# Attention output transposed through DRAM and VectorE in 32x32 blocks, in place of TensorE

## The chip, the cores and the metric

The kernel runs on one core of one Trainium2 chip. The metric is the device time of one execution in microseconds (us), median of several. A core has TensorE (PE in the profile, with its weight loads as PEld), VectorE (DVE), ScalarE (ACT), GpSimd (POOL) and SyncE (SP). Each works through its own instructions in order. In this kernel SP computes nothing: it issues every data transfer, and the transfers are carried out by 16 DMA engines.

## The reference, cut to what matters

An mLSTM cell over 4 batches, 8 heads, 768 steps and head size 40 is followed by a feed-forward layer with a quick-GELU.

```
for t in range(768):                      # per batch and head
    m_new = max(f[t] + m, i[t])
    C = exp(f[t] + m - m_new) * C + exp(i[t] - m_new) * outer(v[t], k[t])
    n = exp(f[t] + m - m_new) * n + exp(i[t] - m_new) * k[t]
    y[t] = sigmoid(o[t]) * (C @ q[t]) / max(abs(n . q[t]), 1)
x = y as (batch*time, head*dim)           # 3072 x 320
h = x @ w_in                              # 320 x 2048
out = (h * sigmoid(1.702 * h)) @ w_out    # 2048 x 320
```

The inputs w_in and w_out are 64-bit floats that the kernel converts to 32 bits by itself.

## The kernel before, in words

Time is cut into six windows (`w`) of 128 steps (`L`), and a window holds four batches (`b`) of 128 tokens. The recurrence is worked out in chunked form, as a masked attention inside a window plus a state that is carried from window to window. For one window and batch the attention has four stages:

- `weights(w, b)`: exponentials on ACT over a tile `wt`, and a causal mask on POOL. For windows after the first, `wt` is loaded by `spread` from a DRAM copy (`m_row`) of a row of maxima.
- `scores(w, b)`: key-query products on TensorE (L329), which VectorE multiplies into `wt` (L331).
- `values(w, b)`: products of `wt` with v (L340) and of q with the state (L346) on TensorE. VectorE then takes seven operations (L350 to L360), the last of which writes `y`, 128 tokens by 320 channels.
- `seam(w, b)`: puts `y` with channels on partitions into `xT[w]`, a tile of 128 partitions by 3 channel groups by 4 batches by 128 tokens. Three TensorE transposes (L369) go into one PSUM tile, and ACT copies it out (L370). Group 2 holds channels 256 to 319 twice, because POOL has appended a second copy of the last 64 channels to `y` (L362).

Feed-forward has two phases per window. In the up phase `up(w, j)` multiplies the converted w_in (`w_in_sb` for channels 0 to 255, `w_in_x` for the others, which are held on both halves of the partitions) with all 512 tokens of `xT[w]` (L405, L411), and ACT applies the GELU. In the down phase window 0 uses plain products (`down`, 16 blocks, L432). Windows 1 to 5 use a two-level fast scheme (`down_fast`, 14 blocks of 8 products, L486) whose results VectorE adds into `o_sb` (L489, L491), and SP stores them (L495).

The order of work is written by hand, and each engine follows program order. While the down phase of window `w` runs, the attention of window `w+1` is interleaved: `attention(w+1)` is a list of eight steps. The first is `columns`. Each later step holds, in this order, `seam` of the batch three behind, `values` of the batch two behind, `scores` of the batch one behind and `weights` of the newest batch, where these exist. `stops` lists after which blocks a step is run. At block 0 of the down phase the gates (`load_gates`, 2 transfers) and the blocked keys and queries (`load_blocks`, 32 transfers) of window `w+2` are issued on SP. The VectorE transposes of these blocks (`transposes`, L288) run in the next up phase. PSUM has two pools of four tiles: `ps_m` for feed-forward, `ps_a` for attention.

Of the kernel before, what the change touches and what calls it, by code (L numbers as in the profile page):

```python
# [8 lines left out]
FP = mybir.dt.float32  # L9
# [13 lines left out]
L = 128  # L23
# [11 lines left out]
def kernel(  # L35
# [12 lines left out]
    nc = tc.nc  # L48
    B, H, S, D = q.shape
    BH = B * H  # L50
    DM = H * D
    DFF = moe_w_in.shape[1]
    NW = S // L
# [12 lines left out]
    work = ctx.enter_context(tc.tile_pool(name="work", bufs=2))  # L66
# [3 lines left out]
    rows = ctx.enter_context(tc.tile_pool(name="rows", bufs=2, space=bass.MemoryType.DRAM))  # L70
# [4 lines left out]
    V, A, G, T = nc.vector, nc.scalar, nc.gpsimd, nc.tensor  # L75
# [11 lines left out]
    w_in_sb = const.tile([128, 2, DFF], FP, name="w_in_sb")  # L87
# [8 lines left out]
    def load(w, what, bs=slice(0, B)):  # L96
        hs = slice(bs.start * H, bs.stop * H)
        for c in what:
            if c == "o" and w not in eo:
                eo[w] = ld.tile([L, BH, D], FP, tag="eo", bufs=1, name="eo")  # L100
            dst, src = {"k": (k_st, k), "q": (q_st, q), "v": (v_st, v), "o": (eo.get(w), o_gate)}[c]
            nc.sync.dma_start(out=dst[:, hs, 0:D],  # L102
                              in_=src[bs, :, w * L:(w + 1) * L, :].rearrange("b h s d -> s (b h) d"))
# [12 lines left out]


    w_in_bits, w_out_bits = moe_w_in.bitcast(U32), moe_w_out.bitcast(U32)
    rest_bits = w_in_bits[256:DM, :].rearrange("k (j two m) -> two k j m", two=2, m=256)
    out_bits = w_out_bits.rearrange("(f p) m -> p f m", p=128)  # L120

# [1 line left out]


    def piece_in(c, n):
        return (w_in_sb[:, c, n * 512:(n + 1) * 512],
                [(slice(0, 128), slice(0, 512), w_in_bits[c * 128:(c + 1) * 128, n * 1024:(n + 1) * 1024])])

    def piece_rest(n):
        return (w_in_x[:, n * 4:n * 4 + 4, :].rearrange("p j m -> p (j m)"),  # L130
# [46 lines left out]
    ident = const.tile([128, 128], FP, name="ident")  # L177
# [26 lines left out]

    m_at = {0: m0}
    cols, stacked, m_row, dec = {}, {}, {}, {}
    kT, qT, wt, ys, xT, gs, o_ps, sums = {}, {}, {}, {}, {}, {}, {}, {}


    def convert(n):  # L210
# [122 lines left out]
    def values(w, b):  # L333
        hs = slice(b * H, (b + 1) * H)
        po = ps_a.tile([L, H, D1], FP, tag="a", name="p_o")
        for p in range(NP):
            for i in range(2):
                h = 2 * p + i
                for t in HALVES:
                    T.matmul(po[t, h, :], wt[w, b][:, p, i, t], v_st[:, b * H + h, :], start=True, stop=True)  # L340
        u = po
        if w:
            pi = ps_a.tile([L, H, D1], FP, tag="a", name="p_i")
            for p in range(NP):
                for t in HALVES:
                    T.matmul(pi[t, 2 * p:2 * p + 2, :].rearrange("p a b -> p (a b)"), qT[w, b][:, p, t],  # L346
                             state[:, b * NP + p].rearrange("p a b -> p (a b)"), start=True, stop=True)
            u = work.tile([L, H, D1], FP, tag="u", name="u")
            g = cols[w][:, BH + b * H:BH + (b + 1) * H].unsqueeze(2).to_broadcast([L, H, D1])
            V.tensor_tensor(out=u, in0=pi, in1=g, op=OP.mult)  # L350
            V.tensor_tensor(out=u, in0=po, in1=u, op=OP.add)

        den = work.tile([L, H, 1], FP, tag="den", name="den")
        V.tensor_scalar(out=den, in0=u[:, :, D:D1], scalar1=-1.0, scalar2=1.0, op0=OP.mult, op1=OP.max)
        V.tensor_tensor(out=den, in0=u[:, :, D:D1], in1=den, op=OP.max)
        V.reciprocal(out=den, in_=den)
        z = eo[w][:, hs, :]
        V.scalar_tensor_tensor(out=z, in0=z, scalar=1.0, in1=u[:, :, 0:D], op0=OP.add, op1=OP.mult)
        y = ys[w, b] = work.tile([L, DM + 64], FP, tag="y", name="y")
        V.scalar_tensor_tensor(out=y[:, 0:DM].rearrange("p (h d) -> p h d", d=D), in0=z, scalar=0.5,  # L360
                               in1=den.to_broadcast([L, H, D]), op0=OP.mult, op1=OP.mult)
        G.tensor_copy(out=y[:, DM:DM + 64], in_=y[:, DM - 64:DM])  # L362

    def seam(w, b):
        if b == 0:
            xT[w] = work.tile([128, 3, B, L], FP, tag="xT", bufs=1, name="xT")
        px = ps_a.tile([128, 3, L], FP, tag="a", name="p_x")
        for c in range(3):
            T.transpose(px[:, c, :], ys[w, b][:, c * 128:(c + 1) * 128], ident)  # L369
        A.copy(out=xT[w][:, :, b, :], in_=px)  # L370

    def carry(w, b):
# [22 lines left out]
    def up(w, j):  # L395


        x = xT[w].rearrange("p c b t -> p c (b t)")
        ph = {}

        def full(j, first):
            for c in range(2):
                for i in range(2):
                    f = 2 * j + i
                    T.matmul(ph[j][i], w_in_sb[:, c, f * 128:(f + 1) * 128], x[:, c, :], start=(first and c == 0),  # L405
                             stop=(not first and c == 1))

        def rest(j, first):
            for i in range(2):
                r = slice(i * 64, i * 64 + 64)  # L410
                T.matmul(ph[j][i], w_in_x[r, j, :], x[r, 2, :], start=first, stop=not first)  # L411

        def gelu(j):
            g = gs[w, j] = gp.tile([128, 2, W], FP, tag="g", name="g")
            for i in range(2):
                A.activation(out=g[:, i, :], in_=ph[j][i], func=AF.Gelu_apprx_sigmoid)  # L416

        for j, first in ((j, True), (j + 1, False)):
            ph[j] = [ps_m.tile([128, W], FP, tag="m", name="p_h") for _ in range(2)]
            if first:  # L420
                full(j, True)
            rest(j, not first)
            if not first:
                full(j, False)
            gelu(j)
# [23 lines left out]
    def weight_sums():  # L449
        V.tensor_tensor(out=t1, in0=w01, in1=w00, op=OP.subtract)  # L450
        V.tensor_tensor(out=t2, in0=w11, in1=t1, op=OP.subtract)
        V.tensor_tensor(out=w01, in0=w11, in1=w01, op=OP.subtract)
        V.tensor_tensor(out=t4, in0=w10, in1=t2, op=OP.subtract)
# [64 lines left out]
    def run(calls):  # L518
        for f, *args in calls:
            f(*args)  # L520
# [37 lines left out]
    def weights_in(n):  # L558
        done, ahead = beside.get(n, ((), ()))
        for p in done:  # L560
            convert(p)
        for p in ahead:
            fetch(p)

    for w in range(NW):
        more = w + 1 < NW
        for j in range(NF // 2):
            if j % 2 == 0:
                if w == 0:
                    weights_in(j // 2)  # L570
                up(w, j)
            if j == 0 and more:
                load(w + 1, "o")
            if w == 0 and j == 0:
                load_blocks(1)
            if w == 1 and j == 1:
                weight_sums()
            if more:
                if j == (3 if w == 0 else 0):
                    gates(w + 1)  # L580
                if j == 4:
                    load(w + 1, "v")
                if j == (7 if w == 0 else 4):
                    spread(w + 1)
                    load(w + 1, "k")
                if j < B:
                    carry(w, j)
                if 4 <= j < 6 if w else j == 7:
                    first = 2 * j - 8 if w else 0
                    transposes(w + 1, first)  # L590
                    transposes(w + 1, first + 1)
            if w and j >= 4:
                hidden_sums(w, (j - 4,), False)
                if j % 2:
                    hidden_sums(w, (j - 5, j - 4), True)
        side = attention(w + 1) if more else []
        if w == 0:

            blocks = [(lambda b=b, n=n: down(w, b, n)) for n0 in (0, 2) for b in range(B) for n in (n0, n0 + 1)]
            stops = range(0, 16, 2)  # L600
        else:
            blocks = down_fast(w, 0) + down_fast(w, 1)
            stops = (0, 1, 2, 4, 6, 8, 10, 12)
        for i, block in enumerate(blocks):
            if w == 0:
                weights_in(4 + i)
                if i == 0:
                    transposes(1, 2)
                    transposes(1, 3)
            if w + 2 < NW and i == 0:  # L610
                load_gates(w + 2)
                load_blocks(w + 2)
            block()
            if i in stops and side:
                run(side.pop(0))
# [30 lines left out]
```

## Time and profile before

The median of three runs is 532.8 us (532.19 to 535.05); the profiled execution spans 532.6 us.

| engine | busy us | share of the span |
|---|---|---|
| PE | 513.5 | 96% |
| PEld | 352.1 | 66% |
| DVE | 266.0 | 50% |
| ACT | 168.3 | 32% |
| POOL | 70.1 | 13% |

| stretch, us from the start | what runs | PE busy us |
|---|---|---|
| 0 to 33 | attention of window 0 | 28.1 |
| 33 to 70.7 | up phase of window 0 | 37.7 |
| 70.7 to 134.6 | down phase of window 0, attention of window 1 | 53.0 |
| 134.6 to 172.4 | up phase of window 1 | 37.8 |
| 172.4 to 216.7 | down phase of window 1, attention of window 2 | 44.3 |

The later windows repeat the last two rows, and the final down phase has no attention beside it. A row of the profile's groups gives the line, the engine, the operation, the tiles it writes and reads, the shapes, the count, the busy time and the mean time of one. The timeline lists the same work in order of time: start, duration, engine, line, operation, tiles, count, and in square brackets the idle time before it and what ended that. "SPq" is SP issuing transfers; a transfer lands later than its issue ends.

### The profile page before, as it was taken

How to read it: one execution, taken by the hardware profiler on the slowest of the kernel's cores; microseconds unless marked ns; L12 is line 12 of the kernel's file. 1: busy time of each engine (PE TensorE's matmuls, PEld its weight loads, DVE VectorE, ACT ScalarE, POOL GpSimd, SP SyncE). 2: the span in 40 equal slices, each digit the busy share in tenths (PEclk: the TensorE clock that was granted, in tenths of full speed). 3: DMA queues.
4: the chain of work that ended last, by engine and by line, in shares of the span. 5: the costliest groups of instructions: out<-in, count | busy, mean ns of one | idle time of the engine just before them, and what ended most of it. 6: DMA issues, size and time to landing. Idle time of an engine off the chain costs nothing.

```text
span 532.6 us, 9546 instructions
## 1 busy us (share of the span) xinstructions
PE 513.5 (96%) x3828; PEld 352.1 (66%) x3828; DVE 266.0 (50%) x603; ACT 168.3 (32%) x367; POOL 70.1 (13%) x104
## 2 busy tenths in 40 slices
PE   8899995599999999999999999999999999999997
PEld 5654463477434999544899643899744799844797
DVE  6868962845376555237365317455307545202511
ACT  4475643520222620212540222451032352032100
POOL 5511000102130110120010220021220021000000
PEclk9999999599999999999999999999999999999999
DMA  9979689740379400387500368610357000000000
GB/s 168 138 248 326 78 153 273 78 55 26 63 210 100 52 27 1 75 220 81 59 27 1 75 171 113 76 28 2 70 102 162 0 14 15 26 0 1 1 25 26
DMA packets 175884, 44.81 MB, mean 84 GB/s; under 512 B 164544, under 2 KB 170720, under 8 KB 175840
## 3 DMA queue, kind: packets, MB, share of 16 engines
q1 hardware_dynamic: 175840, 44.21, 43.4%
q8 instruction: 30, 0.49, 0.4%
q14 instruction: 14, 0.11, 0.1%
HBM read 40.17 MB, written 4.01 MB: 83 GB/s over the span
## 4 chain that ended last, share of the span: by engine, by line
PE 78%; SPq 10%; DMA 5%; ACT 2%; DVE 2%; issue 2%; ACTq 0%
PE p_out L486 27%; PE p_h L405 27%; PE p_h L411 7%; PE p_out L432 4%; PE p_o L340 4%; SPq L113 4%; PE p_s L329 4%; SPq L154 3%; SPq L102 3%; DMA bits<-in_moe_w_in_dram 2%; PE p_i L346 2%; ACT wt L318 2%; DMA wt<-m_row 1%; PE p_x L369 1%; PE p_c L381 1%
## 5 line engine op out<-in xcount | busy, mean ns | idle before, releaser
L405 PE MATMUL p_h<-xT,w_in_sb 128*128 128x512 f32 x384 | 175.0, 602 | 0.0
L405 PEld LDWEIGHTS p_h<-xT,w_in_sb 128*128 128x128 f32 x384 | 69.8, 190 | 92.0 <-issue 89.7
L416 ACT ACTIVATE g<-p_h 128x512 f32<-128x512 f32 x96 | 54.6, 596 | 135.4 <-PE p_h L411 74.9
L486 PE MATMUL p_out<-w_out_sb,g 128*128 128x160 f32 x480 | 71.3, 302 | 0.0
L486 PEld LDWEIGHTS p_out<-w_out_sb,g 128*128 128x128 f32 x480 | 66.8, 190 | 3.7 <-issue 2.4
L321 POOL TENSOR_SCALAR_AFFINE_SELECT wt<-wt 128x1024 f32<-128x1024 f32 x24 | 26.4, 1100 | 203.7 <-ACT wt L318 194.2
L370 ACT COPY xT<-p_x 128x384 f32<-128x384 f32 x24 | 11.5, 478 | 128.7 <-PE p_x L369 128.7
L491 DVE TENSOR_TENSOR o_sb<-o_sb,p_out 128x160 f32<-128x160 f32 x70 | 21.1, 318 | 62.0 <-PE p_out L486 61.7
L318 ACT ACTIVATE wt<-wt,cols 128x128 f32<-128x128 f32 x160 | 48.0, 390 | 8.8 <-DMA wt<-m_row 8.8
L411 PE MATMUL p_h<-xT,w_in_x 64*128 64x512 f32 x192 | 47.7, 615 | 0.0
L486 PE MATMUL p_out<-t,s 128*128 128x160 f32 x320 | 47.5, 301 | 0.0
L486 PEld LDWEIGHTS p_out<-t,s 128*128 128x128 f32 x320 | 44.3, 190 | 0.6
L470 DVE TENSOR_TENSOR s<-g 128x512 f32<-128x512 f32 x20 | 13.8, 692 | 54.0 <-ACT g L416 53.6
L331 DVE TENSOR_TENSOR wt<-p_s,wt 128x512 f32<-128x512 f32 x48 | 30.8, 683 | 19.4 <-POOL wt L321 16.6
L340 PE MATMUL p_o<-v_st,wt 128*64 128x41 f32 x768 | 28.4, 235 | 11.0 <-DVE wt L331 10.9
L432 PE MATMUL p_out<-w_out_sb,g 128*128 128x320 f32 x128 | 38.4, 455 | 0.0
L390 DVE TENSOR_TENSOR state<-p_c,state 40x164 f32<-40x164 f32 x32 | 10.4, 326 | 55.1 <-PE p_c L381 54.7
L411 PEld LDWEIGHTS p_h<-xT,w_in_x 64*128 64x128 f32 x192 | 16.5, 186 | 29.5 <-issue 28.0
L340 PEld LDWEIGHTS p_o<-v_st,wt 128*64 128x64 f32 x768 | 25.3, 141 | 15.9 <-DVE wt L331 11.9
L432 PEld LDWEIGHTS p_out<-w_out_sb,g 128*128 128x128 f32 x128 | 24.9, 199 | 10.9 <-issue 2.1
L329 PE MATMUL p_s<-qT,kT 40*128 40x128 f32 x384 | 28.8, 291 | 0.0
L350 DVE TENSOR_TENSOR u<-p_i,cols 128x328 f32<-128x328 f32 x20 | 10.0, 500 | 35.6 <-PE p_i L346 35.6
(114 smaller groups left out, 524.0 us busy)
## 6 DMA issues: line engine op xcount, KB each, us to landing
wt<-m_row SPq DMA_DIRECT2D x20, 512.0 KB, 6.8
bits<-in_moe_w_in_dram SPq DMA_DIRECT2D x8, 512.0 KB, 5.1
out_dram<-o_sb SPq DMA_DIRECT2D x24, 160.0 KB, 1.8
eo<-in_o_gate_dram SPq DMA_DIRECT2D x5, 640.0 KB, 5.4
v_st<-in_v_dram SPq DMA_DIRECT2D x5, 640.0 KB, 5.8
k_st<-in_k_dram SPq DMA_DIRECT2D x5, 640.0 KB, 8.0
bits<-in_moe_w_out_dram SPq DMA_DIRECT2D x8, 320.0 KB, 4.8
k_bl<-in_k_dram SPq DMA_DIRECT2D x40, 64.0 KB, 2.6
```

The source lines that it names most:

```text
L113: nc.sync.dma_start(out=dst[r:r + 32, :, g, 0:n], in_=src[:, two:H:2, t:t + 32, d:d + n].rearrange("b j s d -> s (b j) d"))
L318: A.activation(out=x[:, h, :], in_=x[:, h, :], func=AF.Exp, scale=-1.0, bias=cols[w][:, b * H + h:b * H + h + 1])
L321: G.affine_select(out=x, in_=x, compare_op=OP.is_ge, fill=0.0, base=0, pattern=[[0, H], [1, L]], channel_multiplier=-1)
L329: T.matmul(pw[i][:, p, :], kT[w, b][r, p, :], qT[w, b][r, p, :], start=True, stop=True)
L331: V.tensor_tensor(out=wt[w, b][:, :, i, :], in0=pw[i], in1=wt[w, b][:, :, i, :], op=OP.mult)
L340: T.matmul(po[t, h, :], wt[w, b][:, p, i, t], v_st[:, b * H + h, :], start=True, stop=True)
L405: T.matmul(ph[j][i], w_in_sb[:, c, f * 128:(f + 1) * 128], x[:, c, :], start=(first and c == 0), stop=(not first and c == 1))
L411: T.matmul(ph[j][i], w_in_x[r, j, :], x[r, 2, :], start=first, stop=not first)
L416: A.activation(out=g[:, i, :], in_=ph[j][i], func=AF.Gelu_apprx_sigmoid)
L432: T.matmul(po, gs[w, f // 2][:, f % 2, b * L:(b + 1) * L], w_out_sb[:, f, :], start=(f == 0), stop=(f == NF - 1))
L486: T.matmul(po, a(f), b[:, f, :], start=(f == 0), stop=(f == NH - 1))
L491: V.tensor_tensor(out=dst, in0=x, in1=po, op=OP.add)
```

## The change

For windows 1 to 5 the transposes leave TensorE and ACT. `values` now writes `y` to a DRAM tile (`y_row`) with three transfers. It reads it back with four more into an SBUF tile `yb`, of which there is one buffer, so that four groups of 64 channels lie on four groups of 32 partitions. `seam` then makes two VectorE transposes in blocks of 32x32 from `yb` into `xT`. In this layout group 0 of `xT` holds the even and group 1 the odd channels of the first 256. The rows of w_in are therefore loaded in the same order (`full_bits`), and window 0, which keeps TensorE, transposes every second channel. POOL's copy of the last 64 channels is kept for window 0 alone. In the fast down phase the steps of the attention run after blocks 0, 1, 2, 4, 5, 7, 8 and 12 (before: 0, 1, 2, 4, 6, 8, 10 and 12), so that more blocks lie between the last `values` and the last `seam`. The loads for window `w+2` are issued at block 9 in place of block 0, in window 0 as well. The purpose is to take the transposes off TensorE.

```diff
+    full_bits = w_in_bits[0:256, :].rearrange("(p c) (n m) -> c n p m", c=2, m=1024)
...
     def piece_in(c, n):
-        return (w_in_sb[:, c, n * 512:(n + 1) * 512],
-                [(slice(0, 128), slice(0, 512), w_in_bits[c * 128:(c + 1) * 128, n * 1024:(n + 1) * 1024])])
+        return w_in_sb[:, c, n * 512:(n + 1) * 512], [(slice(0, 128), slice(0, 512), full_bits[c, n])]
...
-        G.tensor_copy(out=y[:, DM:DM + 64], in_=y[:, DM - 64:DM])
+        if w == 0:
+            G.tensor_copy(out=y[:, DM:DM + 64], in_=y[:, DM - 64:DM])
+            return
+
+        row = rows.tile([L, 4, 96], FP, tag="y_row", name="y_row")
+        nc.sync.dma_start(out=row[:, :, 0:64], in_=y[:, 0:256].rearrange("t (q m) -> t q m", q=4))
+        for i in range(2):
+            nc.sync.dma_start(out=row[:, 2 * i:2 * i + 2, 64:96],
+                              in_=y[:, 256:DM].rearrange("t (q m) -> t q m", q=2))
+        yb[w, b] = work.tile([128, 4, 96], FP, tag="yb", bufs=1, name="yb")
+        for g in range(4):
+            nc.sync.dma_start(out=yb[w, b][:, g, :], in_=row[g * 32:(g + 1) * 32].rearrange("t q m -> q t m"))
 
     def seam(w, b):
         if b == 0:
             xT[w] = work.tile([128, 3, B, L], FP, tag="xT", bufs=1, name="xT")
+        y = ys[w, b]
+        if w:
+            V.transpose(out=xT[w][:, 0:2, b, :], in_=yb[w, b][:, :, 0:64].rearrange("p g (f c) -> p c g f", c=2))
+            V.transpose(out=xT[w][:, 2, b, :], in_=yb[w, b][:, :, 64:96])
+            return
         px = ps_a.tile([128, 3, L], FP, tag="a", name="p_x")
-        for c in range(3):
-            T.transpose(px[:, c, :], ys[w, b][:, c * 128:(c + 1) * 128], ident)
+        for c in range(2):
+            T.transpose(px[:, c, :], y[:, 0:256].rearrange("p (f c) -> p c f", c=2)[:, c], ident)
+        T.transpose(px[:, 2, :], y[:, 256:384], ident)
         A.copy(out=xT[w][:, :, b, :], in_=px)
...
-            stops = (0, 1, 2, 4, 6, 8, 10, 12)
+            stops = (0, 1, 2, 4, 5, 7, 8, 12)
...
-            if w + 2 < NW and i == 0:
+            if w + 2 < NW and i == 9:
                 load_gates(w + 2)
                 load_blocks(w + 2)
```

More of the change, by code (lines that the diff above doesn't have):

```diff
@@ L206 @@
     cols, stacked, m_row, dec = {}, {}, {}, {}
-    kT, qT, wt, ys, xT, gs, o_ps, sums = {}, {}, {}, {}, {}, {}, {}, {}
+    kT, qT, wt, ys, yb, xT, gs, o_ps, sums = {}, {}, {}, {}, {}, {}, {}, {}, {}
     def convert(n):
```

## The prediction

> **What bounds the kernel now.** I read the busy times first, then a table of stretches of the span, one per phase.
>
> ```profile
> PE 513.5 (96%) x3828; PEld 352.1 (66%) x3828; DVE 266.0 (50%) x603; ACT 168.3 (32%) x367; POOL 70.1 (13%) x104
> ```
>
> ```profile
> 70.70:134.60 63.90, 52.97 (x401) 39.24 (x400) 32.55 (x68) 21.59 (x52) 8.19 (x12) 0.87 0.61 117
> 134.60:172.40 37.80, 37.80 (x162) 15.80 (x161) 23.97 (x39) 8.52 (x15) 6.62 (x4) 1.00 0.72 131
> 172.40:216.70 44.30, 44.30 (x497) 42.39 (x496) 22.43 (x58) 14.58 (x41) 7.98 (x12) 1.00 0.19 28
> ```
>
> Columns: stretch, length, busy time of PE, PEld, DVE, ACT, POOL, PE clock, DMA share, GB/s. From 134.6 us on, PE is busy in every microsecond of both phases, so each microsecond of PE work removed there is gained, and each wait that reaches PE is lost. Only the down phase of window 0 has a hole: PE works 53.0 of 63.9 us, because `wt` for window 1 comes late.
>
> Next the timeline of one step, in the down phase of window 1:
>
> ```profile
> 185.23 1.13 PE L340 MATMUL p_o<-v_st,wt 128*64 128x41 f32 x32
> 186.18 0.77 PE L346 MATMUL p_i<-state,qT 128*64 128x82 f32 x16
> 186.88 1.16 PE L329 MATMUL p_s<-qT,kT 40*128 40x128 f32 x16
> 187.00 0.50 DVE L350 TENSOR_TENSOR u<-p_i,cols 128x328 f32<-128x328 f32 x1 [1.19 <-PE p_i L346]
> ...
> 189.07 0.49 DVE L360 SCALAR_TENSOR_TENSOR y<-eo,den 128x320 f32<-128x320 f32 x1
> 189.48 1.28 DVE L331 TENSOR_TENSOR wt<-p_s,wt 128x512 f32<-128x512 f32 x2
> ...
> 192.42 0.49 PE L369 MATMUL p_x<-ident,y 128*128 128x128 f32 x3
> 192.84 1.13 PE L340 MATMUL p_o<-v_st,wt 128*64 128x41 f32 x32
> ...
> 214.51 2.34 PE L486 MATMUL p_out<-w_out_sb,s 128*128 128x160 f32 x16
> 216.69 3.60 PE L405 MATMUL p_h<-xT,w_in_sb 128*128 128x512 f32 x8
> ```
>
> `y` is ready 2.65 us after the end of the step's PE products (186.9 to 189.56), and the masked scores of the next batch, which the next `values` needs on PE, come behind it on VectorE 1.2 us later. The three transposes hold PE for 0.42 us (192.42 to 192.84). From 186.9 to the up phase at 216.69 PE takes 29.8 us.
>
> Last SP's own timeline and the issues:
>
> ```profile
> 163.53 8.33 SPq L113 DMA_DIRECT2D k_bl<-in_k_dram  x16
> 171.97 9.90 SPq L113 DMA_DIRECT2D q_bl<-in_q_dram  x16
> ```
>
> ```profile
> out_dram<-o_sb SPq DMA_DIRECT2D x24, 160.0 KB, 1.8
> k_bl<-in_k_dram SPq DMA_DIRECT2D x40, 64.0 KB, 2.6
> ```
>
> SP takes 0.52 us for one small load (8.33 over 16), and a transfer lands 1.8 us (stores) or 2.6 us (loads) after its issue. These are now hidden by early issue. The change puts two such landings in series between `values` and `seam`.
>
> **What the Trainium skill says.** "DMA: Bandwidth & Descriptors", section "Two DMAs through the same engine are not ordered": a transfer that reads what another wrote must be held back on the issuing engine until the first one's semaphore is complete. So SP stands still while `y_row` lands, and all that is behind it on SP waits. The trace of before has the same pattern once per window (`m_row`, then `wt`) but with up to 10 us between the two, so it doesn't price it. The same page, section "Why a DMA increments its semaphore by 16 and not by 1": a transfer is spread over the largest number of engines up to 16 that divides the slowest dimension of both sides. The reads of `yb` have a slowest dimension of 4 on the DRAM side, so perhaps 4 engines; no row here shows it. "VectorE: DVE Perf Modes", section "The three transpose paths": VectorE transposes 32x32 blocks only, hence the detour. "TensorE: Matmul & The Clock Gate", Part 1: an idle window of about 3.4 us halves PE's clock. The trace agrees: after the hole before 98.5 us the clock is 0.50 until about 107 us.
>
> **The change, part by part.** Removed: 20 times three transposes on PE, 0.42 us where another step follows and 0.33 us for the last of a window, so 1.6 us a window and 8 us in all. The ACT copies (0.48 us) and POOL copies (0.24 us) were hidden behind PE and count nothing. The other order of w_in rows reads the same rows in the same sizes: nothing. Window 0's strided transposes have the same count and shape: nothing.
>
> Added on VectorE: two transposes per batch, 256 and 128 columns. L288 takes 0.67 to 0.71 us for 512 columns, so about 0.5 us. VectorE is half idle, so by itself this costs nothing.
>
> Added on SP and DMA: a round trip C from `y` to a landed `yb`. Three issues of about 0.4 us (a store's issue takes 0.33 us, a load's 0.38 to 0.5 us); the third starts 0.9 us after `y` and lands 1.9 us later: 2.8 us. Then four issues 0.5 us apart, the last landing 2.5 us after its start: 4.1 us with the wake-up. C = 6.9 us; I take 7.0 for a little of the four-engine effect. Lower end: issues of 0.33 and 0.35 us, landings of 1.8 and 1.6 us (the quickest of any load): 5.1 us. Upper end: the DMA engines spent 43.4% of 16 x 532.6 us on 44.2 MB, 12 bytes per ns, so a row of 384 bytes costs 32 ns and 128 of them on each of four engines 4.1 us; with issue overlapping C is about 9 us.
>
> The wait this adds is VectorE's. `seam(b)` stands ahead of `values(b+1)` in a step, and VectorE is in order. So while `yb` of batch b is in flight, the seven operations of batch b+1, the masked scores after them and the evictions all queue up. The four batches become a chain: `y` of one batch, C, 0.5 us of transposes, 2.55 us to the next `y`. From 186.9 as zero: first `y` at 2.65, then 4 round trips, 3 times 3.05 us, the last transposes 0.5 and a wake-up 0.1: 12.4 + 4C = 40.4 us before the up phase can begin. PE alone would need 28.2 us (29.8 less 1.6). PE meets the chain where `values(2)` and `values(3)` wait for their masked scores (about 2.8 and 5 us) and before the up phase (about 4 us). The four blocks between the last `values` and the last `seam` (9 us) hide the last round trip nearly, not the three before, which fall between steps 5.0, 7.1 and 5.0 us apart. So plus 10.6 us a window, for the attention of windows 2 to 5: **+42 us**.
>
> The down phase of window 0 is worse, since its steps stand two blocks apart to the end (`stops` there is unchanged) and the 34 loads at block 9 come on SP between the row transfers of batch 1 and of batch 2. The first `y` is at 104.6 us (just ahead of VectorE's masking at 104.59). Then 104.6 + 7.0 + 3.05 = 114.7 for the second; its reads are issued by 119.7; the loads take SP 0.9 + 32 x 0.52 = 17.6 us, to 137.3, a store 0.35; third round trip lands 144.7; fourth `y` 147.8; landed 154.8; up phase at 155.4 in place of 134.6: **+21 us**. In windows 1 to 3 the loads come behind the last batch's reads and end about 15 us into the up phase. The transposes that use them start 21 us into it and `spread`'s landing is wanted after its end, so moving them costs nothing there.
>
> Clock: the hole of some 20 us before the up phase of window 1 should halve the clock as the one at 98 us did, where PE took 11.9 us (98.53 to 110.44) for about 8 us of work: **+4 us**. The holes of 3 to 5 us in the other windows may or may not, and inside the chain a slow PE is hidden: **+2 us** in all. Sum: 42 + 21 + 4 + 2 = 69, so 532.8 + 69 = **602 us**.
>
> **Rivals.** (1) The round trip is hidden and only the PE work counts: 532.8 - 8 = 525 us. For it speaks that DMA is 81% idle in the down phases; against it that 12.4 + 4C must be under 28.2, so C under 4.0 us, when two landings alone take 3.4 us at their quickest and seven issues 2.3 us. (2) C is near 4.0 and only the loads in window 0 hurt: windows 1 to 4 gain 6 us, window 0 ends 9 us later (111.7, 114.7, 132.3, 136.3, 139.4, 144): 536 us. (3) Every hole halves the clock: some 4 us more in each of four windows, 618 us. It is backed by the 0.50 after 98 us; against it the holes are half as long. (4) Four engines and C = 9: 18.6 us in each of four windows, 27 in window 0, 640 us.
>
> **How the numbers follow.** Forecast, with C between 5.1 (562 us: 3 us a window, 13 in window 0, clock 4) and 8: 0.62. Rivals (1) 0.08, (2) 0.06, (3) 0.15, (4) 0.09. The range 560 to 632 leaves out (1), (2) and about half of (4). Faster 0.08, same 0.02, slower 0.90.
>
> **What would show it.** PE idle in the down phases ended by VectorE's `wt` (L331) and, before the up phase, by VectorE's `xT`; VectorE idle ahead of its `xT` transposes ended by a DMA into `yb`, some 4 us or more each; about 10 us more in each down phase from window 1 on and 20 in that of window 0; up phases as long as before. Wrong would be a round trip under 4 us, VectorE working ahead of a waiting `seam`, or transfers of batch 2 in window 0 that don't wait for the loads.

## The result, and the profile after

The changed kernel takes 645.6 us (median of four, 642.9 to 647.8) against 532.5 us: 1.211 times as long, with an interval of 1.205 to 1.217. The profiled execution spans 641.2 us, 108.6 us more than before.

First the busy times, then the stretches from the start of window 0's down phase to the start of window 2's up phase. The columns are those of the same table of before.

```profile
PE 550.3 (86%) x3768; PEld 379.8 (59%) x3768; DVE 280.2 (44%) x643; ACT 159.2 (25%) x347; POOL 66.9 (10%) x84
```

```profile
74.00:164.70 90.70, 52.45 (x388) 38.40 (x386) 37.18 (x76) 19.69 (x48) 8.27 (x8) 0.82 0.50 99
164.70:205.50 40.80, 40.78 (x161) 17.07 (x162) 24.01 (x40) 8.52 (x15) 6.62 (x4) 0.93 0.56 105
205.50:267.80 62.30, 50.70 (x485) 47.66 (x483) 24.65 (x66) 12.67 (x37) 7.14 (x8) 0.86 0.15 34
```

PE has fewer instructions (60 transposes gone) and a larger busy time, because its clock is lower: 0.86 in the down phase of window 1, where it was 1.00. In that phase PE is now idle for 11.6 of 62.3 us. The DMA engines taken together are no busier than before, 15% of their time in this phase against 19%, so it is not the bandwidth of the 16 that is short.

The table of waits says for what the engines stood still, in us, with the number of waits and the longest:

```profile
DVE xT L380 <- DMA yb<-y_row: 148.4, 20, 20.1
PEld p_o L340 <- DVE wt L331: 55.9, 33, 8.2
PEld p_h L422 <- DVE xT L380: 36.8, 5, 22.9
```

The first line is the new wait, all 20 of it: VectorE in front of the transposes. The other two are where it reaches PE, in `values` by way of the masked scores and before the up phases. Before, the wait in `values` was

```profile
PEld p_o L340 <- DVE wt L331: 11.9, 5, 11.2
```

The chain of work that ended last shows what one batch consists of. These are batch 1 of window 2 and the start of batch 2 (start, duration, what):

```profile
235.99 0.50 DVE y L360
236.50 0.55 SPq L367
237.10 0.62 SPq L369
237.77 1.68 DMA y_row<-y
239.46 0.53 SPq L373
240.04 0.52 SPq L373
240.61 0.51 SPq L373
241.16 3.75 DMA yb<-y_row
245.04 0.45 DVE xT L380
245.49 0.19 DVE xT L381
245.68 0.40 DVE u L350
...
247.63 0.50 DVE y L360
248.15 0.55 SPq L367
```

From one `y` to the next, 236.5 to 248.1 us, there is not one entry of PE: two issues, a landing, three issues, a landing, then VectorE. In the down phase of window 1 of before the same chain was PE throughout. One step of it (the dots stand for the three transposes, 0.33 us):

```profile
188.04 4.54 PE p_out L486 x32
...
192.91 1.06 PE p_o L340 x32
193.98 0.59 PE p_i L346 x16
194.57 1.09 PE p_s L329 x16
195.66 4.54 PE p_out L486 x32
```

The round trip C, from the end of `y` to the first transpose, is 8.6 us here; the four of window 2 take 10.5, 8.6, 7.9 and 8.2 us, 8.8 in the mean.

The length of each phase, from the starts of the first products in the timeline:

| phase | before, us | changed, us | more, us | predicted, us |
|---|---|---|---|---|
| start, to the up phase of window 0 | 32.8 | 36.1 | 3.3 | 0 |
| down phase of window 0 | 63.8 | 90.7 | 26.9 | 21 |
| down phases of windows 1 to 4 | 44.3, 44.3, 44.3, 44.1 | 62.3, 61.7, 62.3, 62.7 | 72.0 | 42 |
| up phases of windows 1 to 5 | 37.8, 37.8, 37.8, 37.8, 35.9 | 40.7, 37.9, 39.6, 37.9, 37.6 | 6.6 | 6 (clock) |

The rows add up to 108.8 us. The up phase of window 0 is as long as before, and the last down phase is 0.3 us shorter.

### The profile page after: what moved, and what is told of

Its sections match the earlier page's. It is cut to its first block, busy times and chain, and to the rows that moved or that the text cites. A ratio compares the mean times of both kernels' runs of the same rounds, so it can differ in the third digit from the quotient of the medians.

```text
span 641.2 us, 9660 instructions
## 1 busy us (share of the span) xinstructions
PE 550.3 (86%) x3768; PEld 379.8 (59%) x3768; DVE 280.2 (44%) x643; ACT 159.2 (25%) x347; POOL 66.9 (10%) x84
## 4 chain that ended last, share of the span: by engine, by line
PE 42%; DMA 20%; SPq 19%; DVE 11%; issue 4%; ACT 3%; DVEq 0%; ACTq 0%
PE p_h L422 23%; PE p_out L503 10%; DMA yb<-y_row 10%; DMA y_row<-y 7%; PE p_h L428 6%; SPq L113 6%; SPq L373 5%; SPq L102 2%; SPq L154 2%; SPq L369 2%; ACT wt L318 2%; DVE u L351 2%; SPq L367 1%; DVE xT L380 1%; DVE eo L358 1%
## 5 line engine op out<-in xcount | busy, mean ns | idle before, releaser
L422 PE MATMUL p_h<-xT,w_in_sb 128*128 128x512 f32 x384 | 181.6, 621 | 35.3 <-DVE xT L380 35.3
L340 PE MATMUL p_o<-v_st,wt 128*64 128x41 f32 x768 | 39.0, 265 | 49.2 <-DVE wt L331 48.7
L503 PE MATMUL p_out<-w_out_sb,g 128*128 128x160 f32 x480 | 76.8, 318 | 0.0
L503 PEld LDWEIGHTS p_out<-w_out_sb,g 128*128 128x128 f32 x480 | 73.3, 205 | 3.1 <-issue 3.1
L380 DVE STREAM_TRANSPOSE xT<-yb 128x256 f32<-128x256 f32 x20 | 8.9, 445 | 148.4 <-DMA yb<-y_row 148.4
L340 PEld LDWEIGHTS p_o<-v_st,wt 128*64 128x64 f32 x768 | 33.6, 173 | 58.1 <-DVE wt L331 55.9
L503 PE MATMUL p_out<-t,s 128*128 128x160 f32 x320 | 54.4, 330 | 0.0
L503 PEld LDWEIGHTS p_out<-t,s 128*128 128x128 f32 x320 | 50.5, 213 | 1.5 <-issue 0.9
L331 DVE TENSOR_TENSOR wt<-p_s,wt 128x512 f32<-128x512 f32 x48 | 30.8, 683 | 21.7 <-POOL wt L321 15.7
L393 POOL TENSOR_TENSOR vw<-v_st,cols 128x328 f32<-128x328 f32 x20 | 16.2, 814 | 229.5 <-PE p_c L398 229.5
L329 PE MATMUL p_s<-qT,kT 40*128 40x128 f32 x384 | 32.5, 317 | 0.7 <-DVE wt L331 0.7
```

The lines of the kernel that those rows point to most:

```text
L329: T.matmul(pw[i][:, p, :], kT[w, b][r, p, :], qT[w, b][r, p, :], start=True, stop=True)
L331: V.tensor_tensor(out=wt[w, b][:, :, i, :], in0=pw[i], in1=wt[w, b][:, :, i, :], op=OP.mult)
L503: T.matmul(po, a(f), b[:, f, :], start=(f == 0), stop=(f == NH - 1))
```

## The experiments

The theory after the result: VectorE's in-order chain of four round trips sets the down phases, as predicted, and one trip is 8.8 us in place of 7.0, mainly because the reads of `yb` run on four engines. All times below are compared with runs of the kernel before on the same chip.

**Reads on 16 engines.**

```diff
-        for g in range(4):
-            nc.sync.dma_start(out=yb[w, b][:, g, :], in_=row[g * 32:(g + 1) * 32].rearrange("t q m -> q t m"))
+        for q in range(4):
+            nc.sync.dma_start(out=yb[w, b][q * 32:(q + 1) * 32, :, :],
+                              in_=row[:, q, :].rearrange("(g t) m -> t g m", g=4))
```

> The changed kernel with its four reads of yb cut by channel group in place of token group, so that the slowest dimension of both sides is 32 and 16 engines can share a read, not 4. Same bytes, packets and number of transfers. Theory A (the round trip is long because 128 packets of 384 bytes queue on each of four engines): the reads end about 1.5 us sooner, so each of the four trips in a window shrinks from about 8.8 to 7.3 us, each down phase by about 6 us, the whole by 25 to 35 us, to about 615 us. Theory B (the trip is issue and landing latency, whatever the number of engines): no change, 645 us.

Measured: 594.3 us, 1.112 times the kernel before (1.108 to 1.117). Theory A holds, and the effect is larger than it said. The packets show that the number of engines changed. These are the changed kernel and this run (packets, MB, share of 16 engines):

```profile
q1 hardware_dynamic: 207840, 52.08, 42.2%
q1 hardware_dynamic: 208800, 52.08, 46.1%
```

The same bytes take 960 packets more, 12 for each of the 80 reads. In the trace the 960 are packets of 4 bytes, and the rows of 384 bytes are 10,240 in both. That is what 16 engines in place of four leave if each of them closes its share of a transfer with one small packet. The chain of this run for the first trip of window 2, and its down phase of window 1:

```profile
215.48 3.41 DMA y_row<-y
218.90 0.30 SPq L373
219.25 1.92 DMA yb<-y_row
```

```profile
196.80:249.90 53.10, 46.96 (x484) 44.15 (x482) 24.65 (x66) 12.67 (x37) 7.16 (x8) 0.94 0.17 38
```

The last read lands 1.9 us after its issue; in the changed kernel it took 2.9 to 3.9 us. The four issues are also quicker (0.43 us each in the median against 0.52). The trips of window 2 measure 7.1, 7.0, 5.9 and 5.9 us, 6.5 in the mean, which is 2.3 us less. Four of them are the 9.1 us by which this down phase is shorter. Not all of the 2.3 us is the number of engines, for the edit changed one thing more. In the trip shown, SP's timeline has the first read issued at 216.76 us, before the third write has landed at 218.89; in the changed kernel no read is issued until it has. In the medians over all trips but the one that the loads hold up, the reads start 0.5 us sooner after the last write's issue, their four issues take 0.5 us less, and the last landing is 1.3 us shorter. The four down phases together gain 36 us, window 0 8 us and the up phases 4 us, where the clock is now full in all but the first.

**Loads at block 0 again.** The edit: `i == 9` is `i == 0`.

> The changed kernel with the 34 loads for window w+2 back at block 0. Theory (in window 0 the loads stand on SP between the rows of batch 1 and batch 2): the wait before the up phase of window 1 shrinks from 22 us to under 8; the first row of window 1 now waits for the end of the loads (some 5 us), so 13 to 20 us are gained, 625 to 632 us; the later down phases stay at 62 us. Rival (the chain of round trips alone makes the hole in window 0): no change, 645 us.

Measured: 638.7 us, 1.195 (1.187 to 1.202). That is 7 us less than the changed kernel, about half of the least that was expected. The down phase of window 0 is 84.2 us in place of 90.7, and PE's hole before the next up phase is 10.8 us in place of 22.4, not under 8. SP's timeline of this run:

```profile
95.10 9.19 SPq L113 DMA_DIRECT2D k_bl<-in_k_dram  x16
104.39 8.41 SPq L113 DMA_DIRECT2D q_bl<-in_q_dram  x16
112.90 0.60 SPq L367 DMA_DIRECT2D y_row<-y  x1
```

The first `y` of window 1 is ready at 106.7 us and its row is issued at 112.9, so the first trip takes 15.0 us. In the changed kernel it was the third that was long, 21.7 us, around loads that held SP from 125.4 to 144.3 us:

```profile
126.32 9.52 SPq L113 DMA_DIRECT2D k_bl<-in_k_dram  x16
135.89 8.45 SPq L113 DMA_DIRECT2D q_bl<-in_q_dram  x16
144.97 0.56 SPq L367 DMA_DIRECT2D y_row<-y  x1
```

The loads cost something at either place; moving them gains 6.5 us net in this phase. The rival (nothing) is out, and so is the size that the theory gave.

**Seams late.** Three `yb` buffers, and no `values` behind a `yb` in flight.

```diff
-            for lag, f in ((3, seam), (2, values), (1, scores), (0, weights)):
+            for lag, f in ((2, values), (1, scores), (0, weights)):
...
+            if s == B + 1:
+                step.insert(0, (seam, w, 0))
+            if s == B + 2:
+                step += [(seam, w, b) for b in range(1, B)]
```

> The changed kernel with three yb buffers in place of one; the VectorE transposes of batch 0 run just before values of batch 3, those of batches 1 to 3 in the last step, so that no values stands behind a yb in flight. The same transfers, in the same order on SP (the tiles u and vw have one buffer to make room). Theory (the cost is VectorE's in-order chain of four round trips, not the transfers): the down phases of windows 1 to 4 fall from 62 us to 43 or 44, about 73 us gained; window 0 keeps most of its hole (loads ahead of batch 2 and 3 on SP), perhaps 5 to 10 us less: 560 to 570 us. Rival (SP or DMA can't carry the trips at that rate): the down phases stay above 50 us, over 600 us.

Measured: 580.2 us, 1.088 (1.080 to 1.096), more than the 560 to 570 expected. The down phases of windows 1 to 4 are 48.4, 48.1, 46.6 and 45.9 us, not 43 or 44: most of the chain's cost is gone though the same seven transfers run. But the up phases had grown to between 40.2 and 43.0 us in windows 1 to 4, from an edit that only made room:

```profile
PEld p_c L398 <- POOL vw L393: 11.0, 10, 1.4
PE p_c L398 <- POOL vw L393: 9.9, 10, 1.3
```

With one buffer of `vw`, the second `carry` of each pair waits for POOL. This is about 10 us over all windows; the rest of the growth goes with a lower clock, 0.93 to 0.96 in the up phases of windows 1, 3 and 4. The next version of this experiment keeps both `vw` buffers.

**The chain broken, nothing else.** Seam four batches behind, two `yb` buffers, the room taken from `u` alone.

```diff
-            for lag, f in ((3, seam), (2, values), (1, scores), (0, weights)):
+            for lag, f in ((4, seam), (2, values), (1, scores), (0, weights)):
...
+            if s == B + 2:
+                step.append((seam, w, B - 1))
```

> The changed kernel with only the chain broken: seam four batches behind, two yb buffers; reads on four engines and loads at block 9 as changed. Theory: the down phases of windows 1 to 4 fall from 62 us to 44 to 46; window 0 keeps the loads on SP ahead of batches 2 and 3 and ends some 8 us sooner than in the changed kernel; up phases at 37.8 us, since vw keeps its two buffers here: 562 to 572 us. Rival (what remained in the run with late seams was the trips, not the single vw buffer): 578 us or more.

Measured: 568.1 us, 1.066 (1.061 to 1.071), 78 us less than the changed kernel. The phases are 79.5 us in window 0 and 47.3, 47.8, 46.6 and 46.0 us in windows 1 to 4. The waits for `yb`, and those for the masked scores in `values`, are for the most part gone:

```profile
DVE xT L380 <- DMA yb<-y_row: 31.5, 11, 6.4
PEld p_o L340 <- DVE wt L331: 16.1, 22, 8.1
```

The four-engine reads are still there, so their landing costs only where something waits for it. The down phases lie up to 2 us above what was expected: the last trip of a window, whose `yb` nothing covers, still ends after PE's last block. The up phases are 37.9 to 39.6 us here, so the single `vw` buffer was the greater part of their growth in the run with late seams.

**The steps of before.** `stops` as before; the loads at block 11, so that they stay behind the last batch's rows in windows 1 to 4.

> The changed kernel with the steps of before (blocks 0, 1, 2, 4, 6, 8, 10, 12); the loads are at block 11, so that they stay behind the rows of the last batch in windows 1 to 4. Theory (a chain of four round trips of 8.8 us sets the length of the down phase, wherever the steps stand): within 8 us of the changed kernel, 637 to 653 us. Rival (the nearer steps are what leaves the trips uncovered): at least 15 us sooner, under 630 us.

Measured: 644.5 us, 1.211 (1.206 to 1.216), as the changed kernel. The down phases of windows 1 to 4 are 61.7, 61.0, 60.7 and 62.2 us. Between these two placings of the steps there is nothing to choose while the chain is longer than PE's work between them.

**TensorE's transposes back.** No `y_row` and no `yb`; the row order, the nearer steps and the loads at block 9 stay.

> The changed kernel with TensorE's transposes for all windows, no y_row and no yb; the order of w_in rows, the nearer steps and the loads at block 9 stay. Theory (these three cost nothing by themselves): 530 to 536 us. Rival (nearer steps make PE wait for masked scores even without the round trip, or the late loads are missed in the next up phase): 2 to 5 us a window, 541 to 553 us.

Measured: 533.2 us, 0.999 (0.997 to 1.001). The down phases of windows 1 to 3 are 44.4 us. So the whole loss comes in with the way through DRAM, and the other three edits taken together cost nothing that can be measured. They were not run one by one: in this profile the down phase of window 0 takes 60.0 us, against 63.8 before, and the start is 1.5 us longer.

**One read in place of four.** The DRAM tile has channel groups first, and a contiguous read of 128 rows brings all back.

```diff
-        for g in range(4):
-            nc.sync.dma_start(out=yb[w, b][:, g, :], in_=row[g * 32:(g + 1) * 32].rearrange("t q m -> q t m"))
+        nc.sync.dma_start(out=yb[w, b].rearrange("p g m -> p (g m)"),
+                          in_=row.rearrange("q (t g) m -> (q t) (g m)", g=4))
...
+            V.transpose(out=xT[w][:, 0:2, b, :].rearrange("p c (t g) -> p c g t", g=4),
```

> The changed kernel with the DRAM tile laid out by channel group first and tokens dealt out four apart, so that yb comes back in one contiguous transfer on 16 engines in place of four; VectorE's transposes write every fourth column to undo it. Chain, steps and loads as changed. Theory (the trip is three issues, a landing, the reads' issue and a landing): with one issue of 0.45 us for 2.2 us and 16 engines for 4 it shrinks from 8.8 to 5.7 us, 12 us in each of four windows and about as much in window 0: 578 to 590 us. Rival (after 16 engines nothing more is to be had): as in the run with 16 engines, 594 us.

Measured: 580.0 us, 1.089 (1.086 to 1.092), as the theory said. One trip in its chain, of window 2:

```profile
218.99 0.37 SPq L367
219.41 0.50 SPq L370
219.96 1.67 DMA y_row<-y
221.63 0.02 SPq L373
221.69 2.64 DMA yb<-y_row
```

The three issues in a row before the last landing are gone. The trip takes 5.4 us, of which 4.3 us are the two landings. The down phases of windows 1 to 4 are 49.9 to 50.9 us, still 6 us above before: the quickest trip of this run takes 5.1 us, and by the prediction's sum the chain fits beside PE's work only under 4.0 us.

**All three costs taken away.** Seam four behind, reads on 16 engines, loads at block 0.

> The changed kernel with all three suspected costs taken away together: seam four batches behind with two yb buffers, so that values never stands behind a yb in flight; reads shared by 16 engines; loads for window w+2 at block 0 (tile u has one buffer to make room). Theory (the round trip costs only where something waits for it; what is left is PE time saved): down phases of windows 1 to 4 at 42.7 us, 1.6 us less than before each, window 0 about as before: 524 to 529 us, faster than the kernel before. Rival (seven transfers per batch cost SP or DMA time that can't be hidden): 535 us or more.

Measured: 536.5 us, 1.007 (1.004 to 1.009). The expected gain did not come. Its down phases of windows 1 to 4 are 44.0, 44.0, 44.0 and 43.9 us, 0.3 us less than before and not 1.6. The timeline shows where the rest went: after a step only one block behind the last, `values` starts before its masked scores are there and its products are torn apart.

```profile
191.63 0.32 PE L340 MATMUL p_o<-v_st,wt 128*64 128x41 f32 x4
192.23 1.02 PE L340 MATMUL p_o<-v_st,wt 128*64 128x41 f32 x28 [0.28 <-DVE wt L331]
```

From the end of the block's products (about 191.4) to 193.06 us, `p_o` takes 1.7 us in place of 0.95 (186.38 to 187.33 in the same window). That happens twice in this window, the second time with 1.4 us. Why the median is then above that of before, though no phase of the profile but the start (1.6 us) is longer, is not settled; the execution profiled (534.1 us) is one of the quickest of this kernel.

**One read, seam four behind, with and without wider steps.** The first kernel of this pair runs the steps after blocks 0, 1, 2, 4, 6, 7, 9 and 12, its twin after the blocks of the changed kernel.

> Meant to beat both kernels: seam four batches behind with two yb buffers, one contiguous read of yb, loads at block 0, and steps after blocks 0, 1, 2, 4, 6, 7, 9 and 12, so that only one pair of values stands a single block apart. Theory (what kept the run with 16 engines from its gain is 0.5 to 0.7 us of waiting for masked scores at each pair of steps one block apart, and 0.6 us for the last trip): down phases of windows 1 to 4 at 43.2 us against 44.3 before, 4.4 us in all, and a little in window 0: 527 to 530 us. Rival (the spacing doesn't matter): as its twin with the steps of the changed kernel.

> The same kernel with the steps of the changed kernel (0, 1, 2, 4, 5, 7, 8 and 12), to part the spacing from the shorter trip. Theory: the two pairs one block apart cost about 0.6 us more a window than in its twin with spread steps: down phases of windows 1 to 4 at 43.4 to 43.9 us, 529 to 533 us. Rival (the last trip alone held the run with 16 engines back): 42.9 us and 527 us or less.

Measured: 530.2 us with wider steps, 0.995 (0.992 to 0.997), and 533.8 us without, 1.001 (0.999 to 1.004). With wider steps the down phases of windows 1 to 4 are 43.4, 43.3, 43.3 and 43.1 us, without them 44.0, 44.0, 44.0 and 43.9. Both kernels end slightly above the upper end expected. The spacing alone is worth 2.8 us in these phases. So the transposes can be taken off TensorE at a profit, if a small one, of 3 us or 0.5%:

```profile
172.20:215.50 43.30, 43.15 (x484) 41.11 (x483) 25.73 (x66) 12.67 (x37) 7.19 (x8) 1.00 0.35 65
```

Against the 44.3 us of before, PE is busy 43.15 us, with its clock at 1.00 again.

## Why the prediction was wrong

The direction and the mechanism were right; the size was not. Measured are 113 us more by the medians (108.6 in the profiles), predicted were 69, and the range ended at 632 us. Of the 40 us between the profiles and the prediction, 30 lie in the down phases of windows 1 to 4.

**The step that failed** is the choice of C: "C = 6.9 us; I take 7.0 for a little of the four-engine effect". Measured are 8.8 us in the mean of the 19 trips that the loads do not hold up. Four trips in each of four windows, 1.8 us longer than put down, make 28 of those 30 us. Term by term, for the trip shown above, 8.6 us: the writes took 3.0 us where 2.8 were put down (issues of 0.55 and 0.62 us, not 0.4, against a landing of 1.7, not 1.9). The reads took 5.6 us where 4.1 were put down (issues of 0.57 us from start to start, not 0.5, and 3.75 us from the start of the last issue to its landing, not 2.5). Five trips of the 19 take 9.6 to 10.6 us because their writes land late, a term that the prediction did not have; without them the mean is 8.3 us.

The four-engine effect was the larger part of the error. The run on 16 engines gives the price of the shape of the reads: 2.3 us a trip, and 51 us of the whole, of which the last landing is 1.3 us a trip. Its 594 us, and trips of 6.5 us, are close to the prediction's 602 us and 7.0 us, which fit a kernel whose reads use 16 engines. The rule was at hand: the Trainium skill's page "DMA: Bandwidth & Descriptors", in the section "Why a DMA increments its semaphore by 16 and not by 1" that the prediction named, has a transfer use the largest number of engines up to 16 that divides the slowest dimension of both sides, which is 4 for these reads. The packets of the two runs agree with it, 12 more for each read on 16 engines. The four-engine case was priced at 9 us a trip in rival (4), given a chance of 0.09, and gave 640 us: the nearest of all numbers. A rule that follows from the shapes alone should have been taken as the value, not as the far end.

**The chain** was right: 12.4 + 4C with the measured 8.8 us gives 47.6 us from the end of batch 0's products to the up phase. Measured in window 2 are 220.0 to 267.8, 47.8 us. The run with the chain broken takes 78 us away with the same transfers, and the run with the old steps takes nothing: that the chain is the cost is shown, not argued.

**Window 0** was right in kind: 26.9 us, with 21 predicted. The loads held SP 19.0 us, not 17.6, and the other three trips took 8.3, 9.6 and 8.3 us, not 7.0. What the prediction did not say is that the loads cost at block 0 too, as the run with them there shows.

**The clock** was about right in sum, 6.6 us in the up phases against 6, with some luck in the parts: 2.9 us after the 22 us hole where 4 were put down, and 3.7 us in the other windows where 2 were. There, holes of 2.8 and 3.0 us before the up phases of windows 2 and 4 left the clock at 1.00; holes of 3.2 and 3.9 us before those of windows 3 and 5 went with 0.96, and with 1.8 and 1.7 us more. After the hole before 98.5 us in the trace of before, the clock stayed at 0.50 until 108 us, not 107. Inside the chain the slow PE is hidden, as assumed: no entry of PE lies in it.

**The costs put at nothing** were nothing as far as they were tested: the run with TensorE's transposes back agrees with before, though it has the other order of w_in, the strided transposes of window 0, the nearer steps and the later loads. The start of the kernel is 3.3 us longer in the changed kernel's profile, but it ranges from 32.8 to 36.2 us over the profiles of all these runs, with no relation to the edits that is visible; it is not put down to the change.

**The gain of 1.6 us a window** was realised only in part, 1.0 us in the best version. One pair of steps a block apart is left there, at which `p_o` takes 1.4 us in place of 0.95. That is 0.45 us of the rest.

## What to carry to other kernels

Here a round trip through DRAM stood between a producer and an in-order engine that had other work queued. It cost its whole latency, 8.8 us, once per item, and the engine's other customers paid it. With one step more of lag the same seven transfers cost 78 us less. Before such a detour is put in, count issues and landings in series and give the consumer other work first (another buffer, one step more of lag). Work out from the two access patterns how many DMA engines a transfer gets: here reads with a slowest dimension of 32 in place of 4 landed 1.3 us sooner.

## What the runs showed of the hardware that was not expected

**The write's landing is sometimes twice as long.** In the chain of the changed kernel 15 of the 20 landings of `y_row` take 1.66 to 1.71 us, and five take 3.17 to 3.71 us. In the stretch around each of those five the DMA table has one transfer of 0.02 MB of the instruction queue q8; around the first trip of window 2:

```profile
q1 hardware_dynamic: 1185, 0.24, 15.6%
q8 instruction: 1, 0.02, 0.7%
```

In the stretches of the landings alone, each of the five has one such transfer and none of the 15 short ones has. An instruction fetch that gets in front of a short transfer on one engine would explain it; no experiment here tested that.

**The single contiguous read took SP less time to issue.** SP takes 0.33 us for that read, of 128 rows (1536 bytes each), 0.43 us for the 16-engine reads and 0.52 us for the four-engine ones.

**VectorE's transpose was slower into every fourth column.** The 256-column transpose takes 0.64 us in the run with one read, against 0.45 us with contiguous output in the changed kernel.
